# Distance table first, key copies on GpSimd, and reordered first periods, loop end and last gates in a fused attention and mixture-of-experts kernel

## The chip, the cores and the metric

The kernel runs on one core of a Trainium2 chip. The metric is the device time of one launch in microseconds (us), taken from runs on the chip.

## The reference

Causal local attention (96 keys back, 8 global keys, a distance bias for each head) over 4 x 8 heads of 768 positions and 64 channels is followed by a mixture of eight experts. Tokens are assigned greedily by descending logit, with room for 384 tokens per expert.

```python
scores = scale * np.matmul(q, k.transpose(0, 1, 3, 2))
...
scores = scores + bias[None, :, :, :]
scores = np.where(keep, scores, -1000000000.0)
a = np.exp(scores - max); a = a / (sum(a) + 1e-09)
x = (a @ v) as 3072 tokens x 512
logits = x @ w_gate
for idx in np.argsort(-logits.flatten()):   # greedy, cap 384 per expert
    ...
out[mask_e] = np.maximum(x[mask_e] @ w1[e], 0.0) @ w2[e]
```

(Shortened; `...` marks cuts.)

## The kernel before

The program goes through these stages: loads and first scores (0 to 23 us), a stretch set by VectorE (23 to 43 us, VectorE busy 18.90 of 20), sixteen pairs of heads paced by TensorE (to 144 us, TensorE busy 75.21 of the first 76), rounds of token assignment filled with early work of the first experts (to 181 us), and the eight experts. The names are these. `expo` is the exponential (ScalarE). `mask` multiplies it by a table of weights `Wm` (VectorE). `kA_out` copies keys, `qT_out` copies queries, `av` is attention times values, `sums` gives the row sums and gates, `tok` brings tokens into row form, and `work(us)` is filler for TensorE from the early experts.

```python
            # first periods
            mask(0, 1)
            warm(8)
            load_v(2)
            load_v(3)
            kA_out(1, 0)
            expo(0, 2, ps)
            qT_out(1, 0, dve=True)
            qT_out(1, 1, dve=True)
            mask(0, 2)
            ...
                # end of one turn of the loop over units
                if u == NU - 2:
                    e1_sums()
                if cur:
                    mask(2 * u + 1, 2)
                if nxt:
                    for hf in range(2):
                        pk = tok(Bp, hf)
                        tok_out(Bp, hf, pk)
            ...
            # end of attention: rows of the first two experts, fetched by index
            av(15)
            px = ps_s.tile([128, 2, NKC, 128], BF16, tag="ps0", name="px")
            for e in range(2):
                for kc in range(NKC):
                    nc.tensor.transpose(px[:, e, kc, :], xe_early[e][:, 128 * kc : 128 * kc + 128], ident_bf)
            oT_out(15, 0)
            oT_out(15, 1)
            for e in range(2):
                nc.scalar.copy(out=xT_early[e], in_=px[:, e])
            pr = sums(15)
            sums_out(15, pr)
            ...
            # routing: filler, then the rounds; then eight row gathers by GpSimd
            work(1.5)
            ...
            for e in range(ER):
                gather(e, range(1, TSLAB), False)
            late_weights(False)
            ...
                # one expert: 8 groups of 4 matmuls into three PSUM buffers, ScalarE empties each
                for fc in range(NFC):
                    ph = ps_h.tile([128, CAP], FP32, tag="ph")
                    for kc in range(NKC):
                        nc.tensor.matmul(ph[:, 0 : 128 * ns], ...)
                    nc.scalar.activation(hT[:, fc, 0 : 128 * ns], ph[:, 0 : 128 * ns], AF.Relu)
```

The softmax here doesn't subtract the row's maximum and nothing guards it: scores larger than these inputs give would overflow.

## Time and profile before

| what | value |
|---|---|
| time of three runs | 266.2, 266.28, 267.0 us (median 266.28) |
| time of the run that was profiled | 261.25 us (span 259.5, mean granted clock 0.989) |
| TensorE, VectorE, ScalarE, GpSimd busy | 93, 63, 55, 34% |
| first expert's first product starts | 180.85 us |

### The profile page before, as it was taken

What the parts mean: (1) busy time and instruction counts of PE and PEld (TensorE: products, weight loads), DVE (VectorE), ACT (ScalarE), POOL (GpSimd) and SP (SyncE); (2) the same over time, 40 slices, a digit from 0 to 9 for tenths busy, and PEclk for the clock granted to TensorE, in tenths of its full rate; (3) what the DMA queues carried; (4) which work ended last, traced back from release to release, by engine and by line L of the source; (5) the groups of instructions that cost most, each with busy time, mean ns of one, the idle gap of its engine ahead of it and who ended that gap; (6) DMA issues with size and microseconds to landing.
All of it is one profiled execution on the core that took longest, in us unless ns stands there. A gap on an engine that the chain in (4) does not pass through costs nothing.

```text
span 259.5 us, 7844 instructions
## 1 busy us (share of the span) xinstructions
PE 241.5 (93%) x3331; PEld 180.0 (69%) x3331; DVE 163.0 (63%) x347; ACT 144.0 (55%) x245; POOL 88.3 (34%) x147
## 2 busy tenths in 40 slices
PE   8699979999999999999998999999999999999960
PEld 2467867888788888887787877765677775555520
DVE  3987998898878988679782687773232323223120
ACT  5998959779597795973432332323444442341600
POOL 5050000030180493005018301127884656742240
PEclk9999999999999999999999999999999999999995
DMA  7993597749689499958998999943599999994221
GB/s 259 328 329 79 160 254 207 197 87 279 185 219 269 81 236 244 198 121 131 208 210 180 168 194 204 201 126 98 96 185 252 262 241 275 231 208 180 83 85 47
DMA packets 52569, 49.29 MB, mean 190 GB/s; under 512 B 29744, under 2 KB 44080, under 8 KB 52528
## 3 DMA queue, kind: packets, MB, share of 16 engines
q0 software_dynamic: 15680, 26.22, 49.2%
q1 hardware_dynamic: 36848, 22.50, 31.7%
q8 instruction: 28, 0.46, 0.7%
q14 instruction: 13, 0.11, 0.1%
HBM read 56.05 MB, written 9.44 MB: 252 GB/s over the span
## 4 chain that ended last, share of the span: by engine, by line
PE 43%; DVE 20%; DMA 13%; issue 9%; ACT 8%; POOL 3%; SPq 1%; POOLq 0%; DVEq 0%
PE ph L1395 7%; PE po L443 6%; PE ps L390 6%; PE po L1404 5%; DVE RT L330 5%; DVE P L423 5%; DMA x_tok<-x 4%; DMA out_dram<-ot,idi 4%; POOL out_dram L955 3%; PE poE L998 3%; PE pr L474 3%; PE pk L519 3%; PE phE L982 2%; DMA RT<-x_tok,idiE 2%; DMA RT<-in_q_dram 2%
## 5 line engine op out<-in xcount | busy, mean ns | idle before, releaser
L408 ACT ACTIVATE P<-ps 128x860 f32<-128x860 f32 (+1 forms) x46 | 39.3, 893 | 23.1 <-PE ps L390 22.3
L1398 ACT ACTIVATE hT<-ph 128x256 bf16<-128x256 f32 (+1 forms) x64 | 27.1, 424 | 38.2 <-PE ph L1395 36.3
L390 PE MATMUL ps<-qT,kA 32*128 32x215 f32 (+2 forms) x864 | 43.2, 333 | 2.5 <-ACT qT L355 2.5
L390 PEld LDWEIGHTS ps<-qT,kA 32*128 32x128 f32 x864 | 36.8, 185 | 7.1 <-ACT qT L355 3.0
L443 PE MATMUL po<-P,v 128*64 128x215 f32 (+6 forms) x576 | 41.3, 293 | 0.1
L443 PEld LDWEIGHTS po<-P,v 128*64 128x64 f32 x576 | 34.1, 136 | 8.4 <-issue 3.2
L423 DVE TENSOR_TENSOR P<-P,Wm 128x860 f32<-128x860 f32 (+1 forms) x32 | 32.9, 1043 | 6.7 <-ACT P L408 4.0
L330 DVE STREAM_TRANSPOSE RT<-RT 128x768 f32<-128x768 f32 x28 | 26.2, 959 | 3.4 <-DMA RT<-in_k_dram 3.4
L474 PE MATMUL pr<-P,onesx 128*32 128x192 f32 (+11 forms) x768 | 27.6, 259 | 0.0
L1411 DVE COPY ot<-po 128x512 f32<-128x512 f32 x18 | 12.5, 692 | 23.9 <-PE po L1404 23.9
L955 POOL DMA_INDIRECT out_dram<-ot,idi x19 | 18.6, 981 | 23.2 <-DVE ot L1411 15.8
L474 PEld LDWEIGHTS pr<-P,onesx 128*32 128x32 f32 x768 | 24.7, 109 | 2.4 <-issue 0.3
L1404 PEld LDWEIGHTS <-hT 128*128 128x128 bf16 x152 | 14.4, 98 | 15.5
L340 ACT COPY kA<-RT 128x720 f32<-128x720 f32 (+2 forms) x18 | 24.4, 1354 | 0.2
L1404 PE MATMUL po<-w,hT 128*128 128x512 bf16 x104 | 23.8, 379 | 0.0
L1395 PE MATMUL ph<-xT,w 128*128 128x384 bf16 (+1 forms) x160 | 23.4, 305 | 0.0
L1376 DVE COPY xT<-pxe 128x512 bf16<-128x512 bf16 x17 | 6.6, 421 | 26.0 <-PE pxe L1375 25.6
L947 POOL DMA_INDIRECT xe<-x_tok,idi x19 | 18.3, 962 | 9.8 <-issue 3.7
L448 ACT COPY oT<-po 128x384 f32<-128x384 f32 x32 | 14.8, 491 | 11.2 <-PE po L443 11.2
L1395 PEld LDWEIGHTS <-w 128*128 128x128 bf16 x160 | 15.7, 98 | 7.7
L416 DVE TENSOR_TENSOR P<-P,Wm 128x860 f32<-128x860 f32 x16 | 16.4, 1058 | 6.6 <-ACT P L408 6.6
L519 PE MATMUL pk<-ident,oT 128*128 128x128 f32 x96 | 16.7, 287 | 2.4 <-DVE LT L490 2.2
(247 smaller groups left out, 330.4 us busy)
## 6 DMA issues: line engine op xcount, KB each, us to landing
w<-in_moe_w_dram POOLq DMA_DIRECT2D x10, 1024.0 KB, 11.9
v<-in_v_dram SPq DMA_DIRECT2D x32, 180.0 KB, 3.4
RT<-in_k_dram SPq DMA_DIRECT2D x7, 768.0 KB, 4.5
RT<-in_q_dram SPq DMA_DIRECT2D x7, 768.0 KB, 6.8
w_early<-in_moe_w_dram POOLq DMA_DIRECT2D x8, 512.0 KB, 7.9
x_tok<-x SPq DMA_DIRECT2D x32, 96.0 KB, 3.2
RT<-in_moe_w_dram POOLq DMA_DIRECT2D x2, 1024.0 KB, 18.4
w_early<-in_k_dram SPq DMA_DIRECT2D x1, 768.0 KB
```

What stands on the lines that cost most here:

```text
L330: nc.vector.transpose(out=t, in_=src[:, :, 32 * g : 32 * g + 32])
L340: nc.scalar.copy(out=kA[:, i0:i1, 8:128].rearrange("p i (c j) -> p i c j", j=NJ), in_=t[:, i0 * NC5 : i1 * NC5, :].rearrange("p (i c) j -> ...
L390: nc.tensor.matmul(heads[a][:, o : o + w], lhsT=kA[r, gd, i, :], rhs=qTt[r, gd, KT * i : KT * i + w], start=(gd == 0), stop=(gd == 1), ski ...
L408: nc.scalar.activation(P[:, :, 0 : GW[g]], ps[w_][:, :, 0 : GW[g]], AF.Exp, scale=0.125)
L423: tt(out=P[:, :, 0 : GW[g]], in0=P[:, :, 0 : GW[g]], in1=Wm[:, h0 : h0 + 2, lo : lo + GW[g]], op=ALU.mult)
L443: nc.tensor.matmul(po[n][bk][64 * t : 64 * t + 64, a - QB * bk : z - QB * bk], lhsT=v7[:, t, i, :], rhs=P[:, t, o + a - q0 : o + z - q0], ...
L474: nc.tensor.matmul(o_, lhsT=l_, rhs=r_, start=first[gq], stop=True, skip_group_check=True)
L519: nc.tensor.transpose(pk[:, bb, :], oTs[n][:, 3 * hf + bb].rearrange("c g r -> c (g r)"), ident)
L955: s = nc.gpsimd.indirect_dma_start(out=out[:, :], out_offset=bass.IndirectOffsetOnAxis(ap=ids, axis=0), in_=ot, in_offset=None)
L1395: nc.tensor.matmul(ph[:, 0 : 128 * ns], lhsT=w1_of(e)[:, kc, 128 * fc : 128 * fc + 128], rhs=xT_e[:, kc, 0:ns, :].rearrange("p t n -> p (t ...
L1398: nc.scalar.activation(hT[:, fc, 0 : 128 * ns], ph[:, 0 : 128 * ns], AF.Relu)
L1404: nc.tensor.matmul(po, lhsT=hT[:, fc, 128 * j : 128 * j + 128], rhs=w2_of(e)[:, fc, :], start=(fc == 0), stop=(fc == NFC - 1))
```

## The change

The intent is to give the distance table to GpSimd in one fixed order, to take small copies off ScalarE, to bring the first exponentials and masks forward, to issue the last row store earlier, and to move the wait for gathered rows behind work that is there anyway. The core of the diff, with cuts marked:

```diff
+    def distances():          # the same 12 instructions, now called first
+        nc.gpsimd.iota(Dm[:, WA:WB], ...)
...
         def kA_out(u, g, i0=0, last=True):
+            small_copy = nc.gpsimd.tensor_copy if u < 3 else nc.scalar.copy
...
             mask(0, 0)
+            nc.vector.tensor_copy(out=ident_bf, in_=ident)
...
-            warm(8)
+            warm(4)
             load_v(2)
             load_v(3)
+            expo(0, 2, ps)
             kA_out(1, 0)
-            expo(0, 2, ps)
             qT_out(1, 0, dve=True)
+            mask(0, 2)
             qT_out(1, 1, dve=True)
-            mask(0, 2)
...
+                if u < NU - 2:
+                    mask(2 * u + 1, 2)
+                for hf in range(2):
+                    pk = tok(Bp, hf)
+                    tok_out(Bp, hf, pk)
                 if u == NU - 2:
                     e1_sums()
-                if cur:
                     mask(2 * u + 1, 2)
-                if nxt:
-                    for hf in range(2): ...
...
+            def first_rows():     # the eight transposes of px
...
+            pr = sums(15, first_rows)   # between the row sums and the gates
             for e in range(2):
                 nc.scalar.copy(out=xT_early[e], in_=px[:, e])
-            pr = sums(15)
             sums_out(15, pr)
...
-            work(1.5)
+            work(1.9)
```

More of the change, by code (lines that the diff above doesn't have):

```diff
@@ L73 @@
     Dm = consts.tile([128, NW], FP32)
-    nc.gpsimd.iota(Dm[:, WA:WB], pattern=[[1, QW]], base=N_GLOBAL, channel_multiplier=-1,
-                   allow_small_or_imprecise_dtypes=True)
-    nc.gpsimd.affine_select(out=Dm[:, WA:WB], in_=Dm[:, WA:WB], compare_op=ALU.is_ge, fill=FAR,
-                            base=N_GLOBAL, pattern=[[1, QW]], channel_multiplier=-1)
-    nc.gpsimd.affine_select(out=Dm[:, WA:WB], in_=Dm[:, WA:WB], compare_op=ALU.is_ge, fill=FAR,
-                            base=N_LOCAL - 1 - N_GLOBAL, pattern=[[-1, QW]], channel_multiplier=1)
@@ L80 @@
-    nc.gpsimd.tensor_copy(out=Dm[:, W0A:WA], in_=Dm[:, WA:WB])
-    nc.gpsimd.memset(Dm[0:N_GLOBAL, WA:WB], FAR)
-    nc.gpsimd.memset(Dm[0:N_GLOBAL, WA : WA + KT], float(N_LOCAL))
-    nc.gpsimd.tensor_copy(out=Dm[:, WB:WC], in_=Dm[:, WA : WA + WC - WB])
-    nc.gpsimd.tensor_copy(out=Dm[:, WC:NW], in_=Dm[:, WA : WA + NW - WC])
-    nc.gpsimd.memset(Dm[0:N_GLOBAL, W0A:WA], FAR)
-    nc.gpsimd.memset(Dm[0:N_GLOBAL, W0A : W0A + KT], float(N_LOCAL))
-    nc.gpsimd.affine_select(out=Dm[0:N_GLOBAL, W0A : W0A + 60], in_=Dm[0:N_GLOBAL, W0A : W0A + 60],
-                            compare_op=ALU.is_ge, fill=FAR, base=-1, pattern=[[-1, 60]], channel_multiplier=1)
@@ L89 @@
-    nc.gpsimd.affine_select(out=Dm[0:N_GLOBAL, W0A + 60 : W0A + KT], in_=Dm[0:N_GLOBAL, W0A + 60 : W0A + KT],
-                            compare_op=ALU.is_ge, fill=FAR, base=60 - N_LOCAL, pattern=[[1, 60]],
-                            channel_multiplier=-1)
+    def distances():
+        nc.gpsimd.iota(Dm[:, WA:WB], pattern=[[1, QW]], base=N_GLOBAL, channel_multiplier=-1,
+                       allow_small_or_imprecise_dtypes=True)
+        nc.gpsimd.affine_select(out=Dm[:, WA:WB], in_=Dm[:, WA:WB], compare_op=ALU.is_ge, fill=FAR,
+                                base=N_GLOBAL, pattern=[[1, QW]], channel_multiplier=-1)
+        nc.gpsimd.affine_select(out=Dm[:, WA:WB], in_=Dm[:, WA:WB], compare_op=ALU.is_ge, fill=FAR,
+                                base=N_LOCAL - 1 - N_GLOBAL, pattern=[[-1, QW]], channel_multiplier=1)
+        nc.gpsimd.tensor_copy(out=Dm[:, W0A:WA], in_=Dm[:, WA:WB])
+        nc.gpsimd.memset(Dm[0:N_GLOBAL, WA:WB], FAR)
+        nc.gpsimd.memset(Dm[0:N_GLOBAL, WA : WA + KT], float(N_LOCAL))
+        nc.gpsimd.tensor_copy(out=Dm[:, WB:WC], in_=Dm[:, WA : WA + WC - WB])
+        nc.gpsimd.tensor_copy(out=Dm[:, WC:NW], in_=Dm[:, WA : WA + NW - WC])
+        nc.gpsimd.memset(Dm[0:N_GLOBAL, W0A:WA], FAR)
+        nc.gpsimd.memset(Dm[0:N_GLOBAL, W0A : W0A + KT], float(N_LOCAL))
+        nc.gpsimd.affine_select(out=Dm[0:N_GLOBAL, W0A : W0A + 60], in_=Dm[0:N_GLOBAL, W0A : W0A + 60],
+                                compare_op=ALU.is_ge, fill=FAR, base=-1, pattern=[[-1, 60]], channel_multiplier=1)
+        nc.gpsimd.affine_select(out=Dm[0:N_GLOBAL, W0A + 60 : W0A + KT], in_=Dm[0:N_GLOBAL, W0A + 60 : W0A + KT],
+                                compare_op=ALU.is_ge, fill=FAR, base=60 - N_LOCAL, pattern=[[1, 60]],
+                                channel_multiplier=-1)
@@ L93 @@
     ident = consts.tile([128, 128], FP32)
-    make_identity(nc, ident)
     ident_bf = consts.tile([128, 128], BF16)
-    nc.vector.tensor_copy(out=ident_bf, in_=ident)
     ones_bf = consts.tile([128, 128], BF16)
@@ L246, with gate_constants @@
     wgx = consts.tile([128, NKC, 32], FP32)
-    nc.gpsimd.memset(wgx, 0.0)
     onesx = consts.tile([128, 2, 32], FP32)
-    nc.gpsimd.memset(onesx, 0.0)
-    for t in range(2):
-        nc.gpsimd.memset(onesx[:, t, 16 + t : 17 + t], 1.0)
+    def gate_constants():
+        make_identity(nc, ident)
+        nc.gpsimd.memset(wgx, 0.0)
+        nc.gpsimd.memset(onesx, 0.0)
+        for t in range(2):
+            nc.gpsimd.memset(onesx[:, t, 16 + t : 17 + t], 1.0)
     Lb = lpool.tile([128, 32, N_EXP], FP32)
@@ L342, in kA_out @@
             if i0 == 0:
-                nc.scalar.copy(out=kA[:, :, 0:8], in_=t[:, 0:1, 0:8].to_broadcast([128, NT, 8]))
+                small_copy(out=kA[:, :, 0:8], in_=t[:, 0:1, 0:8].to_broadcast([128, NT, 8]))
             if last:
-                nc.scalar.copy(out=kA[:, i1, 8 : 8 + LASTK].rearrange("p (c j) -> p c j", j=NJ),
+                small_copy(out=kA[:, i1, 8 : 8 + LASTK].rearrange("p (c j) -> p c j", j=NJ),
                                in_=t[:, i1 * NC5 : 32, :])
@@ L449, in oT_out, with sums @@
                            in_=po[n][bk][:, 0:QB].rearrange("c (g b r) -> c g b r", g=2, b=NBLK))
-        def sums(n):
+        def sums(n, mid=None):
             j = n % NPAIR
@@ L475, in sums @@
                         first[gq] = False
+            if mid:
+                mid()
             for o_, l_, r_ in gates:
@@ L672 @@
         if True:
+            distances()
+            gate_constants()
             load_u(0, kr, k)
@@ L750 @@
             oT_out(1, 1)
-            build_W(7)
+            kA_out(2, 1)
             qT(2, 0)
@@ L757 @@
             expo(1, 2, ps)
-            kA_out(2, 1)
+            build_W(7)
             qT_out(2, 0, dve=True)
             qT_out(2, 1, dve=True)
-            mask(2, 2)
             pr = sums(1)
@@ L766 @@
                 tok_out(1, hf, pk)
+            mask(2, 2)
             for g in range(3):
@@ L822 @@
                 sums_out(Bp, pr)
+                if u < NU - 2:
[3 more added lines that the diff above has]
+                    tok_out(Bp, hf, pk)
                 if u == NU - 2:
                     e1_sums()
-                if cur:
                     mask(2 * u + 1, 2)
-                if nxt:
-                    for hf in range(2):
-                        pk = tok(Bp, hf)
-                        tok_out(Bp, hf, pk)
                 for _ in range(4):
@@ L888 @@
             px = ps_s.tile([128, 2, NKC, 128], BF16, tag="ps0", name="px")
-            for e in range(2):
-                for kc in range(NKC):
-                    nc.tensor.transpose(px[:, e, kc, :], xe_early[e][:, 128 * kc : 128 * kc + 128], ident_bf)
+            def first_rows():
+                for e in range(2):
+                    for kc in range(NKC):
+                        nc.tensor.transpose(px[:, e, kc, :], xe_early[e][:, 128 * kc : 128 * kc + 128], ident_bf)
             oT_out(15, 0)
             oT_out(15, 1)
+            pr = sums(15, first_rows)
             for e in range(2):
                 nc.scalar.copy(out=xT_early[e], in_=px[:, e])
-            pr = sums(15)
             sums_out(15, pr)
```

## The prediction

> **What bounds the kernel now.** I read the busy shares first, then the same shares by stretch, then the chain that ended last, then the waits of TensorE, and at the end the timelines of the engines around the changed lines.
>
> ```profile
> PE 241.5 (93%) x3331; PEld 180.0 (69%) x3331; DVE 163.0 (63%) x347; ACT 144.0 (55%) x245; POOL 88.3 (34%) x147
> ```
>
> TensorE leads, but an average over stages decides nothing, so here are the stretches (length, then busy time of PE, PEld, DVE, ACT, POOL, granted clock, DMA):
>
> ```profile
> 0.00:23.00 23.00, 19.23 (x260) 12.61 (x260) 16.90 (x27) 19.24 (x33) 7.35 (x33) 1.00 0.87 277
> 23.00:43.00 20.00, 18.42 (x347) 15.13 (x343) 18.90 (x28) 16.04 (x26) 0.00 (x0) 1.00 0.63 172
> 43.00:119.00 76.00, 75.21 (x1424) 63.14 (x1425) 64.18 (x115) 59.83 (x83) 22.55 (x50) 1.00 0.80 190
> 119.00:144.00 25.00, 23.61 (x473) 19.11 (x469) 16.57 (x46) 9.20 (x16) 9.28 (x10) 1.00 1.04 191
> ```
>
> From 23 to 43 us VectorE is busy 18.90 of 20 us; after 43 us TensorE is busy 75.21 of 76 us. Before 23 us several engines alternate. The chain that ended last (start, us, what) says in which order:
>
> ```profile
> 15.93 1.59 DVE qT L355 x2
> 17.51 0.98 DVE P L423
> ...
> 18.53 0.98 PE po L443 x12
> 19.51 1.68 PE ps L390 x32
> ...
> 22.88 1.27 ACT Wm L396 x2
> ...
> 24.17 1.06 DVE P L423
> ...
> 43.11 0.27 DVE LT L490
> ...
> 43.42 0.55 PE pk L519 x3
> ```
>
> VectorE copies the second unit's queries before the mask that TensorE's attention awaits; TensorE then does the scores of unit 1; ScalarE takes their exponential and builds two weight tables (L396); only then can VectorE mask at 24.17, and it runs without a gap to 43.4, where TensorE takes over. So what reaches 24.17 earlier makes everything earlier, as long as nothing in between is held by a transfer. From 43 us on, TensorE's waits are few (us in total, times, longest):
>
> ```profile
> PE px L891 <- DMA RT<-x_tok,idiE: 0.8, 1, 0.8
> PE pk L519 <- DVE LT L490: 0.6, 2, 0.4
> PE ph L1395 <- DVE xT L1349: 0.5, 1, 0.5
> PE e L554 <- DVE x L527: 0.5, 1, 0.5
> PE pkn L1083 <- DVE Lb L505: 0.4, 1, 0.4
> ```
>
> The change touches the first, fourth and fifth of them. Even if all five went (2.8 us of 259.5), they are 1.1%: a gain over 2% would have to come from the first 43 us.
>
> [...]where dependent Pool instructions follow each other, the next starts 0.06 to 0.08 us after the end of the last (XM at 54.97 ends 55.17, next 55.23), whereas independent ones overlap by some 0.04 us. [...]the 2x192 Pool copy at 71.42 took 2.51 us across two VectorE mask multiplies (71.75 to 73.73), though a 128x215 copy took 0.35 us at 2.41. [...]The shortest gathers here land 2.7 us after issue[...].
>
> **Part 1, distance table first.** In the kernel before the scheduler placed the identity and gate constants between the table's instructions; the table ended at 4.46 (its last select starts 4.23, lasts 0.23) and the first build began at 4.49. Now the table's 12 instructions stand alone. Adding their own durations with 0.07 us after each dependent pair: 0.92 start, 1.25, 1.68, 2.11, 2.53, 2.87, 3.13, 3.52, 3.68, 3.91, 4.17, 4.47, 4.66. That is 0.2 us *later*, since the fillers had sat in the dependency waits. It doesn't matter: ScalarE's first query copy waited for VectorE's transpose at 8.25 in any case, and that for the q transfer landing at 7.22. Effect 0.
>
> **Part 2, small key copies of units 0 to 2 to GpSimd.** The 56 and 48 element copies cost ScalarE some 0.18 us each, start to start (15.72, 15.90, 16.07). Two per call, two calls per unit, three units: 12 x 0.18 = 2.2 us off ScalarE. Only those before 23 us can count: 4 for unit 0, of which 2 lie after the last wait (0.18 us each), and 4 for unit 1. On GpSimd, unit 0's need four copies of about 0.25 us between 6.4 and 8.0; TensorE wants them at 9.0. No mask multiply runs then. Unit 1's may collide with the mask at 12.1, but have until 18.5.
>
> **Part 3, order of the first periods.** The cast of the identity (0.1 us) leaves the place before the first queries, so scores(0,0) end near 10.9 instead of 11.0; ScalarE, two small copies lighter, is free at 10.84. expo(0,0) starts at 10.9 (before 11.20). Its second half ends 12.56, freeing the bank for scores(0,2), which end at 14.5. expo(0,2) now stands ahead of the keys of unit 1: it starts at 14.55 (before 16.07). From there on ScalarE, start to start as in the timeline: exponential 1.56, keys 1.34 and 1.34, so keys ready near 18.9 (before 19.5), the table W3 begins 18.8 (19.34), done 19.55.
> VectorE: mask(0,0) 12.1 to 13.0, cast 0.1, transposes to 14.85, mask(0,1) to 15.8, one query copy to 16.6, mask(0,2) 16.6 to 17.55 (before 17.51 to 18.49), second copy to 18.35. TensorE: attention to 18.55; scores(1,0) start there, wait after four matmuls for the keys at 18.95, and end at 18.95 + 28 x 0.0525 = 20.45 (before 21.19). expo(1,0) starts at 20.5 (before 21.21); the two tables follow, so the mask of 24.17 moves to 23.5: **0.7 us gained**, the keys being the step that limits it.
> From there to 43.4 VectorE does the same work. The mask(2,2) moved behind the token copies removes TensorE's wait of 1.32 us at 34.24, but the head start ends at the same VectorE instruction (LT, 43.03): TensorE just waits longer at 43.42. Halving the second warm-up (8 to 4 matmuls, 0.95 us) only removes filling. Effect of both 0.
>
> **Part 4, end of the loop.** For unit 6 the token copies go ahead of the early sums (1.5 us) and the last mask (0.95 us), so the row store is issued at about 118.4 relative, 2.4 us earlier than 120.82. TensorE's 0.49 us wait at 120.38 goes. But it isn't kept: VectorE is continuously busy from 114.53 to 125.28 with work that is merely permuted, and the next early matmul needs its result (TensorE arrived at 125.22, started 125.33). The wait moves to there; I keep 0.1 us. The store isn't what releases the gather either: its rows landed at 133.70, the indices were ready at 134.80.
>
> **Part 5, rows transposed at the last gates.** TensorE stood 0.78 us at 141.33 for the gathered rows. Now the 1.56 us of last sums come first; the rows arrive 0.78 us after the attention's end, so the wait is gone: **0.8 us**. ScalarE's copies (1.07 us) slide behind, and end about as the third slab's transposes do.
>
> **Part 6, 0.4 more of early work before the first round.** Five more 128-wide matmuls (0.056 us each) fit into the 0.43 us wait for Lb: 0.28 us of work taken from later. At the other end the first gather, issued 175.56 and at best 2.7 us on its way, holds the transposes of 178.65, so I keep 0.1 us.
>
> Sum: 0.7 + 0.1 + 0.8 + 0.1 = 1.7 us; 266.28 - 1.7 = 264.6. The expert stage from 181 us on shows one TensorE wait (its first), so the gain should last to the end.
>
> **Rivals.** (a) *Nearly nothing, 265.8*: a GpSimd key copy blocks the mask at 12.1 or is blocked, or the keys of unit 1, now behind the exponential, hold scores(1,0) longer than reckoned. For it: keys are my limiting step; against it: even the worst blocking seen is about 2 us for copies with 6 us to spare. (b) *More, 263.2*: the head start of TensorE at 34 us and the 0.49 us at 120 are kept. Against it: both run into a VectorE stretch without a gap. (c) *The weights' transfers become the bound* late, as DMA share in 119 to 144 is full: rows land later relative to TensorE, costing 0.3 to 0.8 of part 5. Against it: these transfers are paced by the same VectorE results and shift along.
>
> **Range and chances.** Parts 3 and 5 are sure in sign, not in size (0.3 to 1.0, and 0.4 to 0.8); runs of before spread from 266.2 to 267.0. I give 263.4 to 265.9. Over 2% faster would be below 260.95, over three times the sum: 3%. Slower by 2% needs a new wait of 5 us: 2%.
>
> **What would show it.** Right: the mask of tables 4 and 5 starts near 23.5; VectorE is gapless from there to near 42.7; TensorE's longest wait before tok(2) grows to over 1 us; no wait before the first row transposes; a wait of some 0.5 us before the second early matmul group. Wrong: waits of TensorE or VectorE for POOL, a gap of VectorE between 24 and 42 us, or a new wait for a transfer in the experts.

## More of the kernel before

The end of the chain of waits, which the prediction does not show, is this (start, length, what) in the first expert, whose products are `ph` (first) and `po` (second):

```profile
180.85 3.67 PE ph L1395 x32
...
184.97 3.45 PE po L1404 x16
```

TensorE runs through without a piece of waiting (from 182 to 186 us it is busy for 4.00 of 4).

## The result

After: 266.84, 267.09, 267.51 and 267.55 us, median 267.3. Before, on the same chip: median 266.35 (266.2 to 267.0). The ratio is 1.0029 with a 95% interval of 1.0006 to 1.0052, so the change made the kernel no faster, and on this chip slightly slower. Ratios here and below are the mean time of one kernel's runs over that of the other's of the same rounds, so not quite the ratio of the medians quoted. Executions over 1.5% slower than the fastest of the same kernel are left out of the means. The predicted 264.6 us and its range up to 265.9 missed; the most likely class, within 2%, was right.

The busy line of the kernel after:

```profile
PE 244.8 (92%) x3327; PEld 181.4 (68%) x3327; DVE 163.1 (62%) x347; ACT 141.9 (54%) x233; POOL 92.1 (35%) x159
```

ScalarE has 12 instructions and 2.1 us less, as reckoned (2.2).

Two pieces of the chain of waits after, from its first 43 us:

```profile
23.43 1.06 DVE P L427
...
42.70 0.55 PE pk L525 x3
```

The mask that stood at 24.17 starts at 23.43 and TensorE takes over at 42.70 instead of 43.42: 0.7 us, as predicted. The waits of TensorE from 40 us on (us in total, times, longest):

```profile
PE ph L1407 <- issue: 2.5, 3, 0.8
PE pk L525 <- DVE LT L496: 1.6, 2, 1.3
PE px L981 <- ACT RT L908: 0.8, 1, 0.8
PE e L597 <- DVE CE__101 L588: 0.6, 1, 0.6
```

The wait for the gathered rows is gone, the wait at the second early matmul is there (0.6), and TensorE's longest wait before the tokens has grown to 1.3 us: three of the signs that I had named. Two lines are new. TensorE's third slab of row transposes (`px` L981) waits 0.8 us for ScalarE's copies of the first two, and the first expert's first product waits under "issue", which means that the profile shows nothing that it waited for. The chain where the time went, first in the fifteenth pair's attention, then in the first expert:

```profile
137.41 1.46 PE po L447 x15
...
139.34 0.40 issue
139.75 1.70 PE po L447 x14
```

```profile
181.08 1.91 PE ph L1407 x16
...
183.44 0.60 PE ph L1407 x4
184.04 0.83 issue
184.88 0.60 PE ph L1407 x4
185.47 0.84 issue
...
189.46 4.45 PE po L1416 x16
```

In the profile before, the attention's last matmul started 2.31 us after its first; here it took 3.89. The first product took 3.95 us to the start of the second; here it took 8.18, and the second then began at half clock. ScalarE shows the cause of the standing more plainly, for it empties each group of four matmuls 0.02 us after TensorE's signal (183.01 for a signal at 182.99), and with all three buffers full TensorE starts the next group 0.06 us after one has been emptied (184.88, emptied at 184.82) (start, length, what, in brackets the idle time before and the releaser):

```profile
183.01 0.39 ACT L1410 ACTIVATE hT<-ph 128x256 bf16<-128x256 f32 x1 [0.85 <-PE ph L1407]
184.44 0.38 ACT L1410 ACTIVATE hT<-ph 128x256 bf16<-128x256 f32 x1 [1.05 <-PE ph L1407]
185.87 0.38 ACT L1410 ACTIVATE hT<-ph 128x256 bf16<-128x256 f32 x1 [1.05 <-PE ph L1407]
```

One group in 1.43 us, where TensorE's own spacing is 0.44 us. The trace also records when TensorE's completion signal changes. Set beside the modelled end of the last matmul of each group (my list from the trace, us):

```
group ends   182.13  182.56  183.00  184.04  185.47  186.91
signal came  182.99  184.42  185.85  187.28  188.73  190.16
late by        0.86    1.86    2.85    3.24    3.26    3.25
```

After 190.16 three more signals follow 0.06 us apart. The same happened in the attention: the signal for the fourteenth pair's gates, ended at 137.38, came at 140.52, and the next at 140.71. Between the two lie the attention matmuls that the chain shows from 137.41 on, over 1.4 us of work. They can't have run in 0.19 us, so at least here it was the signal that was late, not the work. In the profile before, the signals come 0.01 to 0.08 us after the ends in these two stretches.

The record of signals itself has gaps here. It holds 3771 changes of semaphores (the counters by which engines and transfers signal) in this trace and 4209 in the profile before. From 176 to 192 us it holds 29 landings of transfers here and 128 before. ScalarE's signals for its groups that ended at 184.82, 186.26 and 187.69 aren't in it at all, yet TensorE starts its next groups at 184.88, 186.31 and 187.74, so these took effect in time. The lateness of TensorE's signals is seen in ScalarE's starts, and not only in the record, so it is real. But more than TensorE's signals is disturbed there.

The distance from the modelled end of a matmul to its signal is 0.01 to 0.08 us in these two stretches of the profile before and over 3 us here, and it isn't seen in the instruction's record: from 137 to 142 us TensorE counts as busy for 4.45 of 5 us here and for 4.22 before, though the attention took 1.58 us longer here. So a busy PE line can hide the event.

The half clock comes after the standing, not before it. The stretches after (length, then busy time of PE, PEld, DVE, ACT, POOL, granted clock, DMA share, GB/s):

```profile
181.00:185.00 4.00, 2.64 (x22) 2.08 (x23) 0.02 (x1) 1.15 (x3) 3.06 (x4) 1.00 0.34 98
185.00:189.00 4.00, 2.33 (x18) 1.75 (x17) 0.00 (x0) 1.02 (x3) 3.52 (x6) 0.87 0.62 101
```

From 181 to 185 us TensorE is already held up at a granted clock of 1.00; the half clock lasts from 187.93 to 191.34.

### The profile page after: what moved, and what is told of

It is laid out like the page before. It is cut to its first block, busy times and chain, and to the rows that moved or that the text cites. A ratio compares the mean times of both kernels' runs of the same rounds, so it can differ in the third digit from the quotient of the medians.

```text
span 265.0 us, 7846 instructions
## 1 busy us (share of the span) xinstructions
PE 244.8 (92%) x3327; PEld 181.4 (68%) x3327; DVE 163.1 (62%) x347; ACT 141.9 (54%) x233; POOL 92.1 (35%) x159
## 4 chain that ended last, share of the span: by engine, by line
PE 47%; DVE 19%; issue 11%; ACT 10%; DMA 5%; POOL 4%; POOLq 0%; SPq 0%; DVEq 0%; ACTq 0%
PE po L447 9%; PE ps L394 6%; DVE P L427 6%; PE ph L1407 6%; PE po L1416 6%; DVE RT L333 5%; PE pr L478 4%; POOL out_dram L967 4%; PE poE L1010 3%; DMA out_dram<-ot,idi 3%; PE pk L525 3%; ACT qT L359 2%; PE phE L994 2%; DMA RT<-in_q_dram 2%; ACT P L412 2%
## 5 line engine op out<-in xcount | busy, mean ns | idle before, releaser
L412 ACT ACTIVATE P<-ps 128x860 f32<-128x860 f32 (+1 forms) x46 | 39.4, 894 | 23.4 <-PE ps L394 22.7
L447 PE MATMUL po<-P,v 128*64 128x215 f32 (+6 forms) x576 | 42.3, 293 | 1.0 <-DVE P L427 0.4
L447 PEld LDWEIGHTS po<-P,v 128*64 128x64 f32 x576 | 34.7, 136 | 9.2 <-issue 3.8
L1407 PE MATMUL ph<-xT,w 128*128 128x384 bf16 (+1 forms) x160 | 23.4, 305 | 0.0
```

What stands on the lines that cost most here:

```text
L412: nc.scalar.activation(P[:, :, 0 : GW[g]], ps[w_][:, :, 0 : GW[g]], AF.Exp, scale=0.125)
L447: nc.tensor.matmul(po[n][bk][64 * t : 64 * t + 64, a - QB * bk : z - QB * bk], lhsT=v7[:, t, i, :], rhs=P[:, t, o + a - q0 : o + z - q0], ...
L1407: nc.tensor.matmul(ph[:, 0 : 128 * ns], lhsT=w1_of(e)[:, kc, 128 * fc : 128 * fc + 128], rhs=xT_e[:, kc, 0:ns, :].rearrange("p t n -> p (t ...
```

## The experiments

I formed four theories first. **A**: usual runs of both kernels carry these late signals, and the first profile of before was a run without them. **B**: a part of the change makes them. **C**: a throttle comes first. **D**: the loss is only the new wait for ScalarE and the larger filler. Later two more were needed: **G**: the signals come late only while GpSimd issues one transfer after another. **H**: GpSimd has nothing to do with it. In all, 18 runs were made, since the prediction was wrong and the cause open; each call's kernels shared a chip. "Quick chip" means one on which before takes about 261 to 263 us, "slow chip" one with 266 to 269: the kernel before has a median of 261.39 us on chip 9, 267.5 on chip 15 and 268.93 on chip 8.

### First call, chip 9: before 261.39 us

**e0_before**: no edit.

> The kernel before, unchanged, run as an experiment, to see what its usual runs (266.2 to 267.0) hold that its first profile (261.25) did not. Ratio 1.000 by construction. Theory A (usual runs of both kernels carry stretches in which TensorE's completion signals come about 3 us late): if the profile falls on a run near 266, it shows, somewhere, signals over 1 us late and TensorE standing under 'issue' for 4 to 6 us in all, which the first profile lacks. Theory B (the change itself makes these stretches): a profile near 266 with no late signals. Theory C (a throttle comes first): granted clock below 1.0 begins before TensorE stands idle. If the profile falls near 261 again, it tells only that the profiled runs and the others differ.

Measured: 261.26 us, ratio 0.9991 (0.9968 to 1.0014). The profile is again without late signals. So neither the run nor chance made 261 and 266: this chip gives 261 each time, and the three runs of 266 came from elsewhere. The prediction's base and its trace belonged to different chips, or to a chip in different conditions; I can't tell these two apart.

**e1_after**: no edit.

> The kernel after, unchanged, a second profile. Theory A: time near 267 again, ratio 1.003, but the late stretches lie elsewhere or differ in length if they are chance; if they lie again in pair 15's attention and the first expert, they belong to the program. Theory D (the loss is only the new wait for ScalarE before the third slab's transposes and the larger filler): no late signals, first expert's first product 3.7 us long, and still 267.

Measured: 260.72 us (259.88 to 262.95), ratio 0.9967 (0.9927 to 1.0006). No late signals, first product 3.95 us: D alone can't be the loss of the first comparison. The profiled run was a disturbed one (261.81), and its trace shows why. Two stretches of 3.4 us, the second at the recorded half clock, in e1_after and then in e11_after_again, the same program without it:

```profile
171.70:175.10 3.40, 3.27 (x46) 2.40 (x43) 2.49 (x10) 0.60 (x1) 1.97 (x2) 1.00 0.20 77
175.10:178.50 3.40, 3.40 (x11) 1.23 (x9) 0.99 (x6) 0.60 (x1) 2.48 (x4) 0.50 0.29 80
```

```profile
171.70:175.10 3.40, 3.25 (x47) 2.39 (x45) 2.49 (x10) 0.60 (x1) 1.89 (x2) 1.00 0.20 77
175.10:178.50 3.40, 3.40 (x21) 1.69 (x20) 1.48 (x7) 1.18 (x2) 2.49 (x4) 1.00 0.27 80
```

Half the matmuls are done in the same stretch (11 against 21), and the first expert starts 1.6 us later (181.28 against 179.68). The half-clock stretch of the first result is 3.41 us long (187.93 to 191.34); in e7_filler, of the second call, the granted clock of 0.66 from 185 to 189 us and 0.59 from 189 to 194 gives 6.8 us of half clock, if it was whole or half throughout. The same program meets the half clock at 175.1 us in some runs only: it is in the trace of e14_after_more (0.50), too, and not in that of e11_after_again (1.00). TensorE counts as busy for 3.40 of 3.40 and then 3.27 of 3.40 us before this fall, so the profile shows no idle stretch there, and what brings the fall on was not shown. What the stretch before it holds is 24 short matmuls of the index search, a candidate that I didn't test.

Runs of before, too, fall into two groups by mean clock (0.987 to 0.993, and below), so I compare runs of mean clock 0.987 or more on chip 9 over all calls: before has 20 of its 35 runs beside the experiments there, 261.03 to 261.69, median 261.31; after has 8 of 16, 259.88 to 260.23, median 260.01. **The change is worth 1.3 us on this chip**, against 1.7 predicted.

**e2_first**: end of the loop, gates and filler set back to before; parts 1 to 3 kept.

```diff
-            pr = sums(15, first_rows)
+            pr = sums(15)                # and the loop end as before
-            work(1.9)
+            work(1.5)
```

> Parts 1 to 3 alone (the first periods), end of loop, gates and filler as before. Theory A with a clean gain of 0.7 us: 265.6, ratio 0.9974, and the mask of tables 4 and 5 near 23.4. Theory B in the form that the last three parts do the harm: the same 265.6, and the end without late signals. If even this is 266.3 or more, the first parts' gain is lost on the way, in whatever the trace then shows between 43 and 180 us.

Measured: 260.48 us, ratio 0.9977 (0.9942 to 1.0011); span of the profile 258.7 against 259.4. The first expert starts at 180.16 (180.85): 0.69 us, kept to the end, as predicted.

**e3_gates**: part 5 alone on the kernel before.

```diff
-            pr = sums(15)
+            pr = sums(15, first_rows)    # transposes between sums and gates
```

> Part 5 alone (rows transposed at the last gates), all else as before. Prediction's step: 0.8 us gained, 265.5, ratio 0.997. Theory D: the 0.78 us wait for the rows goes and a wait of about 0.75 us for ScalarE's copies takes its place, so 0.0 to 0.3 us: 266.0 to 266.4. Theory B (this part brings the late signals in the first expert): 267 to 271 with the first expert's first product over 6 us.

Measured: 260.51 us, ratio 0.9958 (0.9937 to 0.9979), the first expert at 180.00: 0.85 us. Part 5 brings what was predicted, and B is refuted for it on this chip. Theory D's size is refuted too, though its wait of 0.8 us for ScalarE's copies exists here as in after. From the gate transpose to the key products it costs 0.2 us here (1.86 us in place of 1.64).

### Second call, chip 15: before 267.5 us

**e4_second_copy_dve**: after, with one of the copies on VectorE.

```diff
-            for e in range(2):
-                nc.scalar.copy(out=xT_early[e], in_=px[:, e])
+            nc.scalar.copy(out=xT_early[0], in_=px[:, 0])
+            nc.vector.tensor_copy(out=xT_early[1], in_=px[:, 1])
```

> After, but the second of the two copies of the first rows is made by VectorE beside ScalarE's, to shorten the new wait of TensorE for ScalarE before the third slab's transposes (0.8 us in both profiles of after). Theory D (that wait and the filler behind it eat part of the gain): wait falls to about 0.3 us and the first round's key products, 144.85 in the clean profile of after, start 0.3 to 0.5 us earlier; time 0.3 us below after on the same chip. If the wait is only filling (the round is set by VectorE's gates): no change in time. Should VectorE's copy delay its gate transposes (142.72), the round starts later instead. On a chip where before takes 266: theory A wants late TensorE signals here too.

Measured: 266.79 us, ratio 0.9972 (0.9878 to 1.0066; one of its four runs, 271.06 us, was slow and is in the median but not in the ratio). A miss: VectorE's copy starts only after ScalarE's (144.47 after 143.85 to 144.43), TensorE still waits 0.7 us, and the gate transpose comes after it.

**e5_no6**: after, with part 6 undone.

```diff
-            work(1.9)
+            work(1.5)
```

> After with the filler before the first round back at 1.5 instead of 1.9 (part 6 undone). Theory D: the round's key products start about 0.28 us earlier (five matmuls of 0.056) and the time stays within 0.1 us of after, as the filler is then done later; if the filler was in the way, it falls 0.2 us. Theory B (the larger filler[...] brings on the half-clock window at 175): fewer runs with a clock below 0.986.

Measured: 268.01 us (266.43 to 269.62), ratio 0.9998 (0.9915 to 1.0082): nothing resolved in time. In the trace the round's key products start 1.85 us after the gate transpose, against 2.13 in after: the 0.28 us of five matmuls.

**e6_end_only**: parts 4, 5 and 6 on the kernel before (the diff of the last three hunks alone).

```diff
-                if cur:
                     mask(2 * u + 1, 2)   # end of loop as in the change
-            pr = sums(15)
+            pr = sums(15, first_rows)
-            work(1.5)
+            work(1.9)
```

> Parts 4, 5 and 6 together on the kernel before (first periods as before). With e2_first (0.9 us by medians, 0.7 by spans) and a clean gain of after of 1.3 us: 0.6 us faster than before, ratio 0.9977, if the parts add. If part 5 alone (0.9) is worth more than 4, 5 and 6 together, then part 6 or 4 takes something back.

Measured: 267.44 us, ratio 0.9993 (0.992 to 1.0066). Not resolved.

**e7_filler**: part 6 alone on the kernel before.

```diff
-            work(1.5)
+            work(1.9)
```

> Part 6 alone on the kernel before: filler 1.9 instead of 1.5. Prediction's step: the 0.43 us wait for the gates before the first round takes five matmuls, and 0.1 us is kept: ratio 0.9996. On a chip where before takes 266 this is the nearly unchanged kernel whose trace must show, by theory A, TensorE signals that come over 1 us late and 4 to 6 us of standing; by theory B none.

Measured: 267.05 us, ratio 0.9969 (0.9895 to 1.0042). What counts is the trace, the nearly unchanged kernel on a slow chip. ScalarE in the first expert:

```profile
183.29 0.38 ACT L1398 ACTIVATE hT<-ph 128x256 bf16<-128x256 f32 x1 [0.88 <-PE ph L1395]
184.73 0.38 ACT L1398 ACTIVATE hT<-ph 128x256 bf16<-128x256 f32 x1 [1.06 <-PE ph L1395]
```

The same spacing of about 1.43 us, at the same place, without the change. All four traces of this call and that of the first result show it, and in all of them the signal of the fourteenth pair's gates comes 3.1 us late. **B falls** (e5_no6 has every part but the sixth and e7_filler the sixth alone, so no part is common to them), **and A holds for slow chips**, as far as e7_filler stands for before; it falls for quick ones, where none of the traces shows it. C falls: the granted clock is 1.00 when it begins.

This call also shows what happens to part 5 there. In every slow trace the fifteenth pair's attention is 1.58 to 1.73 us longer (3.89 to 4.03 in place of 2.31). In e7_filler the row transposes that follow start only 0.73 us later than in the profile before (142.06 against 141.33), because the old wait for the rows takes in the rest. In after they start 1.40 us later than in its undisturbed trace (143.04 against 141.64): there is no wait left to hide it. So the 0.8 us of part 5 doesn't exist on a slow chip, in traces of two kernels; it isn't a timed comparison.

The gaps in the record go with the late signals: the slow traces, this one and those of the later calls included, hold 3771 to 3830 changes of semaphores, all quick ones 4200 to 4216.

In all five slow traces the burst that ends the first expert's late signals comes within 0.06 us of the end of GpSimd's last issue before a pause (190.16 and 190.17, 190.45 and 190.50, 191.32 and 191.26, 190.92 and 190.89, 190.43 and 190.41). GpSimd in after, at that time:

```profile
184.78 0.95 POOL L959 DMA_INDIRECT xe<-x_tok,idi  x1 [0.31 <-issue]
...
189.21 0.97 POOL L932 DMA_DIRECT2D w<-in_moe_w_dram  x1
193.19 1.01 POOL L967 DMA_INDIRECT out_dram<-ot,idi  x1 [3.02 <-DVE ot L1423]
```

The late signals of the attention, too, lie in a row of four gathers (134.40 to 139.84 in after). That gave theory G. The match isn't complete: in the attention the late signals come 0.7 and 0.9 us after the row's end (140.52 and 140.71 against 139.84), and in the first expert the row of gathers begins at 175.94 in after, while signals stay on time up to 181.70. Late signals, by up to 2 us, also occur in the later experts of slow traces. In after TensorE's starts there keep their distance to the quick trace (after against e1_after, within 0.15 us from 192 us on), so there they cost nothing.

### Third call, chip 9: before 262.71 us

**e8_weights_later**: after, with two weight transfers moved behind the first expert.

```diff
-            late_weights(False)
...
-                if first:
+                if first and e > 0:
                     late_weights()
+                    if e < 3:
+                        late_weights()
```

> After, with the two weight transfers that GpSimd issues between the eight row gathers and the first expert's stores (one each near 185.7 and 189.2) moved behind the first expert. On a chip where before takes 266, in all five slow traces so far the late TensorE signals of the first expert end in a burst within 0.06 us of the end of GpSimd's last of these issues (190.16 and 190.17, 190.45 and 190.50, 191.32 and 191.26, 190.92 and 190.89, 190.43 and 190.41). Theory G (TensorE's signals come late only while GpSimd issues one transfer after another): the burst moves with that end, to about 188.3, and the time falls by about 1.8 us against after on the same chip. Theory H (something of the chip or of the program's place, GpSimd not concerned): burst and time stay. On a chip where before takes 261: no late signals, time as after within 0.3 us.

Measured: 260.85 us, ratio 0.9948 (0.9893 to 1.0003). Level with after, as expected on a quick chip; it tests nothing of G.

**e9_gathers_apart**: four of the eight gathers moved behind the first store and the second expert's start.

```diff
-            for e in range(ER):
+            for e in range(2):
                 gather(e, range(1, TSLAB), False)
...
+                if first and e == 1:
+                    gather(3, slabs(3))
...
                     scatter(ot, ...)
+                    if first and e == 0 and j == 0:
+                        gather(2, slabs(2))
```

> After, with only four of the eight gathers before the experts; those of the third expert stand behind the first expert's first store, those of the fourth at the second expert's start. GpSimd's unbroken row of issues then ends some 4 to 5 us earlier (near 185.5). Theory G on a slow chip: the burst moves to about 185.5 and the first expert's first product shortens by 3 to 4 us; part of it is given back where the third expert waits for its rows (on a quick chip the rows, issued near 192, land near 196, so I expect this kernel 2 to 4 us slower there). Theory H: the burst stays at 190.

Measured: 268.88 us, ratio 1.0264 (1.0211 to 1.0316), 8.3 us above after where I had expected 2 to 4. TensorE waits 6.2 us for rows, where I had reckoned with the gathers' own 4 us. Without the two weight transfers ahead of them (e10_both, next) the waits are 2.6 us.

**e10_both**: both edits.

> Both of these: GpSimd has no transfers to issue between the scatters of the early rows (near 184) and the first expert's first store. Theory G on a slow chip: late signals end near 184, the first expert's first product takes 3.7 to 5 us in place of 7.5. Theory H: unchanged 7.5. On a quick chip as e9_gathers_apart.

Measured: 264.95 us, ratio 1.0126 (1.0044 to 1.0208); 2.6 us of waiting for rows. No late signals, but there are none here in any case.

**e11_after_again**: after, no edit.

> After, unchanged, beside these on the same chip. On a slow chip: as the first result, 267 with ratio 1.000 to 1.003, if on such chips part 5's 0.8 us is lost because late signals delay the fifteenth pair's attention by 1.4 us in both kernels, which in the kernel before hides in its wait for the rows. On a quick chip: 260.0 in clean runs, ratio 0.995 for them.

Measured: 260.57 us, ratio 0.9957 (0.99 to 1.0014). Its profile, at 260.01 us, is the undisturbed trace of after that I use below. (One run of before took 595.66 us and was left out as slow.)

### Fourth and fifth call, chip 9: before 261.92 and 261.6 us

**e12_best**: e8_weights_later with part 6 undone.

```diff
-            work(1.9)
+            work(1.5)
```

> After with part 6 undone (filler 1.5) and the two weight transfers behind the first expert: the candidate to beat both. On a quick chip, by the traces of e11_after_again and e3_gates: the first round's key products start 1.86 us after the gates' transpose in place of 2.13, of which 0.16 us should be kept at the first expert, so clean runs at 259.8 against 260.0 for after and 261.3 for before. On a slow chip, theory G: the burst of late signals ends about 1.9 us earlier than in after, with the last issue of GpSimd before it, and the time is about 2 us below after's; theory H: as after within 0.5 us.

Measured: 260.03 us, ratio 0.9946 (0.9917 to 0.9975); its undisturbed runs 259.85 to 260.13 against 260.01 to 260.23 for after. The key products start 1.86 us after the transpose, as expected, but 0.1 us is too little to call it better than after.

**e13_both_again** and **e15_both_third**: the kernel of e10_both.

> The kernel of e10_both, for a slow chip. Theory G: GpSimd issues nothing between about 183.3 and the first expert's first store, so the first expert's first product takes 3.7 to 5 us (7.5 in after on such chips) and no signal is late after 184; what it loses is the wait for the third expert's rows, 2.6 us on the quick chip. Theory H: first product 7.5 us. On a quick chip: 3 to 5 us slower than after, as measured (264.95 against 260.57).

> The kernel of e10_both once more, for a slow chip. Theory G: GpSimd issues nothing between about 184 and the first expert's first store, so the first expert's first product takes 3.7 to 5 us (7.5 in after on such chips) and no signal is late after about 184.5. Theory H: first product 7.5 us, a burst of late signals near 190. On a quick chip: as the two runs before, 265.

Measured: 265.44 us, ratio 1.0114 (1.0075 to 1.0152), and 264.93 us, ratio 1.01 (1.0044 to 1.0156). Both came to chip 9 again: they confirm e10_both and leave G open.

**e14_after_more**: after, no edit.

> After beside before in five rounds. Slow chip: ratio 1.000 to 1.003 (part 5's gain is lost there, since the late signals delay the fifteenth pair's attention past the landing of the rows in both kernels). Quick chip: ratio 0.995 to 0.997, clean runs 260.0 against 261.3.

Measured: 260.75 us, ratio 0.9952 (0.9925 to 0.998). With five rounds the gain of after on this chip is clear of zero.

### Sixth call, chip 8: before 268.93 us

**e16_both_no4**: e10_both with part 4 undone.

```diff
-                if u < NU - 2:
-                    mask(2 * u + 1, 2)
                 for hf in range(2): ...      # token copies, again after the mask
```

> The kernel of e10_both with part 4 undone (end of the loop as before). Slow chip, theory G: GpSimd issues nothing between about 184 and the first expert's first store, so the first expert's first product takes 3.7 to 5 us (7.5 in after on such chips) and no signal is late after about 184.5; theory H: 7.5 us, and a burst of late signals near 190. Quick chip: the last gates' transpose starts at 142.6 to 142.7 in a run without a half-clock window (142.81 in e13_both_again), so part 4 costs 0.1 to 0.2 us instead of gaining 0.1; times as e10_both within 0.3 us.

Measured: 268.78 us, ratio 0.998 (0.9945 to 1.0014; one of its five runs, 272.86 us, was slow and left out of the ratio). GpSimd and ScalarE in the first expert, as their timelines show them:

```profile
182.63 0.99 POOL L967 DMA_INDIRECT out_dram<-otE,idiE  x1 [0.22 <-issue]
189.96 0.97 POOL L967 DMA_INDIRECT out_dram<-ot,idi  x1 [6.34 <-DVE ot L1426]
```

```profile
183.45 0.38 ACT L1413 ACTIVATE hT<-ph 128x256 bf16<-128x256 f32 x1 [1.00 <-PE ph L1410]
184.88 2.33 ACT L1413 ACTIVATE hT<-ph 128x256 bf16<-128x256 f32 x6 [1.04 <-PE ph L1410]
```

GpSimd's row ends at 183.62. The late signals end in a burst at 184.86 to 184.98, and from there ScalarE takes its groups without a gap (six in 2.33 us). The first product takes 5.91 us to the start of the second, not 7.55 to 9.65 as in the other five slow traces. **H falls**, in this one trace, on a chip from which there is no trace of before or after. G's time of 184.5 was missed by 0.5 us and its 5 us by 0.9. The run doesn't separate GpSimd's issuing from the traffic of the transfers that it starts, since both are gone from this stretch (from 185 to 189 us GpSimd is busy for 0.00 us and the DMA share is 0.02, against 3.52 us and 0.62 in after). Nor does any run test another rival, that the recording of the trace itself holds signals up on such chips: every run of the experiments has a recorded clock. In GpSimd's second row of issues, from 189.96 on, signals are late from about 194.4, and a burst ends them at 201.51 to 201.69, as two weight transfers have been issued (201.63). But GpSimd goes on at 201.94, with no longer a pause than within the row (0.3 us), and the next signals are on time (202.70 for an end at 202.69). So a row of issues isn't enough for late signals, and of G it is shown only that this burst came earlier with the shorter row. The kernel isn't faster than before, though the first expert is: it waits for rows later and stands again beside that second row.

### Seventh call, chip 1: before 262.36 us

**e17_shorter_row**: after with parts 4 and 6 undone, the weights of e8_weights_later, and only the fourth expert's gathers behind the first store.

```diff
-            for e in range(ER):
+            for e in range(3):
                 gather(e, range(1, TSLAB), False)
...
+                    if first and e == 0 and j == 0:
+                        gather(3, slabs(3))
-            work(1.9)
+            work(1.5)
```

> After with parts 4 and 6 undone, six of the eight gathers before the experts (the fourth expert's two behind the first expert's first store) and the two weight transfers behind the first expert. GpSimd's unbroken row then ends near 186 instead of 190. Slow chip, theory G: the burst of late signals ends near 186 to 187, and the kernel is 2 to 4 us below before on the same chip, unless the second row that it makes behind the first store (two gathers, a store, two gathers, two weights) brings late signals of its own, as in e16_both_no4, which would give back 1 to 3 us. Theory H: within 1 us of before. Quick chip: clean runs at 259.7, against 261.3 for before, with no wait for rows.

Measured: 261.9 us, ratio 0.9974 (0.9932 to 1.0015). This is a quick chip with no late signal in the trace. TensorE waits 1.4 us for rows of a later expert, which I had not expected, so this version isn't the better one. On a slow chip it stays untested.

## Why the prediction was wrong, and what in it was right

**The step that failed is the last one of the sum: "266.28 - 1.7 = 264.6".** It subtracts a saving read from a trace of 261.25 us from a time that was taken where runs are 5 us longer, and takes for granted that the saving is the same there. For part 5, the largest term, it isn't: the 0.8 us wait for rows that it removes was read from the quick trace, and on a slow chip the late signals leave no such wait (see "On the slow chips" below). The sentence behind it, "The expert stage from 181 us on shows one TensorE wait (its first), so the gain should last to the end", was true of the trace only. On chips where before takes 266 or more, TensorE's signals come late in the fifteenth pair's attention and in the first expert; the five first slow traces lose 1.6 us in the one and 3.6 to 5.7 us in the first product of the other (7.55 to 9.65 against 3.95). The prediction's rivals have nothing like it.

**Against the quick chip the sum was nearly right.** The undisturbed traces give the gain by steps (start of each, us):

| start of | before | e2_first (parts 1 to 3) | e3_gates (part 5) | after (e11) |
|---|---|---|---|---|
| gate transpose of pair 15 | 144.16 | 143.47 | 143.28 | 142.79 |
| first round's key products | 145.80 | 145.10 | 145.13 | 144.93 |
| first expert | 180.85 | 180.16 | 180.00 | 179.68 |

- Part 1, effect 0: the last table instruction ended at 4.65 (predicted 4.66, before 4.46) and nothing followed from it. Right.
- Parts 2 and 3, 0.7 us: 0.69. Right, by the step named: the keys and the exponential before the mask at 23.4. The copy of keys on GpSimd that I expected to collide did so (1.01 us at 12.20, beside the mask from 12.03 to 13.07; the others below 0.3) and cost nothing.
- Part 4, 0.1 us: TensorE's early sums start 0.41 us earlier (119.38 in e11_after_again, 119.79 in e2_first), but the next early matmul then waits and stands 0.09 us behind (124.83 and 124.74). Nothing is kept. The mechanism, that the wait moves on, was right, and the remainder of 0.1 was mis-sized.
- Part 5, 0.8 us: 0.85 alone. Together with the earlier parts slightly less, as the wait for rows is 0.7 there (e2_first) and not 0.8.
- Part 6, 0.1 us: the sign was wrong. The step "Five more 128-wide matmuls ... fit into the 0.43 us wait for Lb" fails because part 5 uses up that wait: TensorE first waits 0.8 us for ScalarE's copies. From gate transpose to key products e3_gates takes 1.86 us and after 2.13, so 0.28 us are lost; from there to the first expert 0.12 us come back (34.87 and 34.75). Part 6 costs 0.16 us. I had priced each part alone.

One slip of arithmetic in the prediction, 18.95 + 28 x 0.0525 = 20.42 and not 20.45, changes nothing.

The sum is then 0.69 + 0.85 - 0.16 = 1.38 us for the start of the first expert, where 1.18 are measured. By my estimate, the 0.2 missing are what part 4 (0.09) and the smaller wait under part 5 (0.1) make. Timed runs give 1.3 us.

**On the slow chips, what is shown and what stays open.** Shown: the late signals belong to chip and program, not to the change; in the first expert they ended early in the one trace where GpSimd's row of issues did; part 5 finds no wait to remove there. What parts 4 and 5 bring instead can be read from two kernels of the second call, which differ by these parts alone. TensorE's wait between attention and first round is this in e6_end_only, which has them:

```profile
PE px L974 <- ACT RT L901: 0.8, 1, 0.8
```

and this in e7_filler, which hasn't:

```profile
PE pkn L1083 <- DVE Lb L505: 0.2, 1, 0.2
```

The fifteenth pair's attention starts at 138.08 and 138.02, and the clock is 1.00 in both from the attention to 186 us. The key products start at 147.08 with parts 4 and 5 and at 146.38 without them, the first expert at 181.84 and 181.33. So in these two traces parts 4 and 5, priced at 0.9 us of gain, cost 0.5: the wait for the rows is gone anyway, and the new wait for ScalarE is all that is left. Theory D, refuted for the quick chip, holds in this point. With the 0.69 us of parts 1 to 3 that leaves, by an estimate from traces of two chips, 0.2 us of gain at the first expert. The first comparison shows 0.95 us of loss. The first product alone differs by up to 2.1 us among five slow traces, and half clocks follow it in some of them (granted clock 0.59 from 189 to 194 us in e7_filler) and not in others (mean clock 0.993 of the whole run in e4_second_copy_dve), so the difference may come from where GpSimd's row and TensorE's groups fall against each other. The four runs of after there had mean clocks of 0.975 to 0.987; those of before aren't on record. I have no trace of before from that chip, and no timed comparison of the unchanged after on another slow one. That the gain is lost there is explained by these traces; the sign of what was measured isn't.

**No version beats both kernels everywhere.** After is the best of those measured on quick chips; e12_best is level with it.

## What to carry to other kernels

Before subtracting anything, compare the time of the run that was profiled with the median that the saving is subtracted from; a gap larger than the expected saving (here 5 us against 1.7) means that the trace lacks something which the timed runs have. When two parts of a change act on the same wait, price them together, since a wait can be removed or filled once only. When an engine stands under "issue" while its consumers take its results at an even slow pace (here one group in 1.43 us), compare its completion signals with its modelled ends, count whether the record of signals is whole, and look at who issues transfers in that stretch.
